# Two weight units loaded later, eight high parts on VectorE, other banks for the last chunks, two states faded on GpSimd

## The chip, the cores and the metric

The kernel runs on one core of one Trainium2 chip. The metric is device time in microseconds (us). TensorE multiplies matrices, VectorE and ScalarE read and write both memories, GpSimd works on SBUF alone, and SyncE issues all loads and stores in one queue. In the profile they are PE, DVE, ACT, POOL and SP; PEld is TensorE's weight load.

## The reference

```python
def _attn_ref(q, k, v, lam):          # B=2, H=8, S=768, D=64
    ...
    for b in range(nb):               # blocks of 64
        intra = np.einsum('bhic,bhjc->bhij', qb, kb) * Dmask[None]
        intra = np.einsum('bhij,bhjd->bhid', intra, vb)
        inter = np.einsum('bhid,bhde->bhie', qb * lam_pow[None], kv_state)
        out[:, :, sl] = intra + inter
        kv_state = lam_block * kv_state + np.einsum('bhsd,bhse->bhde', kb_dec, vb)

x = attn_out as tokens x features     # 1536 x 512
h = x @ w_in;  g = h * np.tanh(softplus(h));  x = g @ w_out      # 512 -> 2048 -> 512
h = x @ w_in2; g = h * clip(h + 3, 0, 6) / 6; out = g @ w_out2
```

## The kernel before

**Attention.** The tokens are worked on in 12 chunks of 128 (0 to 5 are the first batch, 6 to 11 the second), each with all eight heads. A chunk `c` takes these steps on TensorE: `update(c)` makes the new state from k and v (L232), `scores` of a later chunk k times q (L188), `attend(c)` masked scores times v (L240) and, but for a batch's first chunk, the old state times q (L246). VectorE multiplies scores by the decay mask (`weigh`, L214). `tokens(c)` splits the chunk's result into a high part (`split_hi`, L102, ScalarE) and a low part, what the rounding to the matmul's format left out (`split_lo`, L106, VectorE). `carry(c)` adds the faded state and the update (L257, VectorE) and fades the new one for the next chunk in four activations (L262, ScalarE). GpSimd scales k by reverse powers (`scale_k`, L200) and q by powers (`scale_q`, L204). A chunk's raw data is loaded in two halves of 512 KB (q and k for the scores, then k and v), four chunks ahead, when the chunk that used the buffer is done.

**Weights.** The weights of the first feed-forward layer come in units: tile `t` of 128 features (16 of them), half 0 (for the first product) or 1 (for the second), one or two tiles at a time. A unit is loaded as 64-bit words (L301), made into a single float in `to_single` (two ScalarE steps at L324, through one scratch buffer `tops`, and VectorE's merge of bits, L327), and split into a high (L102, ScalarE) and a low part (L108, VectorE) in `finish`. `plan` is their order; `start_next` begins the next one, `finish_next` splits it and then issues the loads that `MADE_FIRST` allows by then: the load at place i is issued when that many units are finished. Single units lie in three slots of `ring`, double ones and the pair in `SHARED` in the two buffers `st2`.

**Feed-forward.** Step `n` runs `gemm1` (the first product, 12 matmuls of 128x512, L358) for one tile of features and `emit_g2(n - 2)` (the second product, 12 matmuls, L367) for the tile two steps before. `act_first` evaluates the activation twice on ScalarE (L387, L388), `g_lo` makes its low part on VectorE. Steps 0 to 7 are the first 512 tokens with the lower eight tiles, which need the first twelve entries of `plan`. The second layer follows from 309 us on with fast matrix multiplication (L738, L755).

**What sets the order.** While an engine is in `held`, its instructions stay in the order in which the code writes them, the whole attention stage and the first steps through. From step `LOOSE` on, `held` is empty and the compiler's planner orders each engine's instructions, by their place in the code and by when it thinks them ready.

**PSUM** has eight banks: "h" 0 and 1, "y" 2 to 5, "a" 6 and 7; `gemm1` writes "h", the first `emit_g2` 2 to 5.

Of the kernel before, what the change touches and what calls it, by code (L numbers as in the profile page):

```python
# [14 lines left out]
U64 = mybir.dt.uint64  # L15
ACTF = mybir.ActivationFunctionType
# [6 lines left out]
def decay_attention__mish_ffn__hswish_ffn_kernel(  # L23
# [170 lines left out]
    def follows(c):  # L194
        return c % CPB > 0
# [56 lines left out]
    def carry(c):  # L252
        if carries(c):
            u = uo_t[c][0]
            new = state[(c + 1) % 2]
            if follows(c):
                hold("vector", nc.vector.tensor_tensor(out=new, in0=faded, in1=u, op=ALU.add))  # L257
            else:
                hold("vector", nc.vector.tensor_copy(new, u))
            if carries(c + 1):  # L260
                for p in range(4):
                    hold("scalar", nc.scalar.activation(  # L262
                        out=faded[:, p], in_=new[:, p], func=ACTF.Copy, scale=lampow[:, p, 127:128],
                    ))

    def tokens(c):
        o = uo_t[c][1]
# [4 lines left out]
    stage_t = {}  # L272

    unit_turn = [0]
    SHARED = [(0, 1), (3, 0)]
    shared = []
    busy = set()
    slots = {}

    def load_w(w, t, half, count):  # L280
        if w is w1 and count == 2:
            st = stage_p.tile([128, 2, 512], U64, tag="st2", name="st")
        elif w is w1 and (t, half) in SHARED:
            if not shared:
                shared.append(stage_p.tile([128, 2, 512], U64, tag="st2", name="st"))
            i = SHARED.index((t, half))
            st = shared[0][:, i:i + 1]
        elif w is w1:
            i = unit_turn[0] % 3
            unit_turn[0] += 1  # L290
            slots[w is w1, t, half] = {i}
            st = ring[:, i:i + 1]
        else:
            i = unit[t // 2, half] % 2
            slots[w is w1, t, half] = {0, 1} if i == 0 else {3}
            st = ring[:, 0:2] if i == 0 else spare[0][:, 16:24].bitcast(U64).rearrange("p (t i) n -> p t (i n)", t=2)
        taken = slots.get((w is w1, t, half), set())
        assert not taken & busy
        busy.update(taken)
        words = w[t:t + count, half].rearrange("t p n -> p t n").bitcast(U16)  # L300
        ins = nc.sync.dma_start(out=st.bitcast(U16)[:, :, 0:2047], in_=words[:, :, 1:2048])  # L301
        if w is w1:
            follow(ins)
        stage_t[w is w1, t, half] = st
# [5 lines left out]
    RANGE = 2.0 ** 8  # L310
    tops = []

    def to_single(st, dest=None):

        rest, head = (st.bitcast(I32).rearrange("p t (n c) -> p t n c", c=2)[..., i] for i in range(2))
        if not tops:
            tops.append(tm1_p.tile([128, 600], F32, tag="th", name="tops"))
        n = st.shape[1] * st.shape[2]
        half, bits = (
            tops[0][:, 0:n // 2].bitcast(d).rearrange("p (t n) -> p t n", t=st.shape[1]) for d in (F16, I16)  # L320
        )
        bf = st.bitcast(BF16).rearrange("p t (n c) -> p t n c", c=4)[..., 2]
        for o, i, scale in ((half, bf, 0.5), (head, bits, 65536.0)):
            ins = nc.scalar.activation(out=o, in_=i, func=ACTF.Copy, scale=scale)  # L324
            if dest is not None or "scalar" in held:
                tc.keep_in_program_order(ins)
        hold("vector", nc.vector.scalar_tensor_tensor(  # L327
            out=head if dest is None else dest.bitcast(I32), in0=rest, scalar=13, in1=head,
            op0=ALU.logical_shift_right, op1=ALU.bitwise_or
        ))  # L330
        return st.bitcast(F32).rearrange("p t (n c) -> p t n c", c=2)[..., 1]

    def split(hi, lo, src, scale=1.0):
        split_hi(hi, src, scale)
        split_lo(lo, hi, src, scale)

    single = {}

    def begin(w, t, half, count):
        single[t, half] = to_single(staged(w, t, half))  # L340

    def finish(w, t, half, count):
        hf = single.pop((t, half))
        cols = slice(half * 512, half * 512 + 512)
        if count == 2:
            whole, i = (lowB, t) if t < 3 else (lowA, t - 3)
            both = whole.rearrange("p (t a n) -> p t a n", a=2, n=1024)[:, i:i + 2, :, cols]
            split(both[:, :, 0], both[:, :, 1], hf, RANGE)
        else:
            for i in range(count):  # L350
                split(W[t + i][:, 0:1, cols], W[t + i][:, 1:2, cols], hf[:, i:i + 1], RANGE)

    PASS = ((0, 0), (0, 1), (1, 0))

# [125 lines left out]
                units.append((w, tiles[i - lead], 1, 1))  # L480
        return units

    plan = [(w1, t, half, 1) for t, half in ((0, 0), (1, 0), (2, 0), (0, 1), (3, 0), (1, 1))]
    plan += [(w1, 4, 0, 2), (w1, 2, 1, 1), (w1, 3, 1, 1), (w1, 6, 0, 2), (w1, 4, 1, 2), (w1, 6, 1, 2)]
    NLOW = len(plan)
    MADE_FIRST = [0, 0, 0, 0, 0, 1, 1, 2, 3, 5, 7, 10]
    plan += order(w1, range(HALF, NF))

    loaded = [5]
# [2 lines left out]

    begun = [0]

    def start_next():
        begin(*plan[begun[0]])
        begun[0] += 1

    def finish_next():
        finish(*plan[done[0]])  # L500
        done[0] += 1
        while loaded[0] < limit[0] and done[0] >= (
            MADE_FIRST[loaded[0]] if loaded[0] < NLOW else loaded[0] - 1
# [81 lines left out]
    weigh(0)  # L585
    scale_k(1, "vector")
    for c in range(NCH):
        update(c, "h" if c % 2 == 0 else "a")
        if c < 4:
            scores(c + 1, "y")  # L590
        attend(c)
# [1 line left out]
            scores(c + 2, "y")  # L593
        if c < NCH - 2:
            weigh(c + 1)
        if c == NCH - 3:
            weigh(c + 2)
        if c < NCH - 1 and follows(c + 1):
            scale_q(c + 1, "gpsimd" if c else "vector")
        tokens(c)  # L600
        carry(c)
        if c < NCH - 2:
            scale_k(c + 2)
        if c == 9:
            finish_next()
        if c in (8, 10):
            start_next()
        if c == 4:
            load_w(*plan[0])
        if c < NCH - 4:  # L610
            load_raw(c + 4, 0)
            if c == 7:
                load_w(*plan[1])
            load_raw(c + 4, 1)
        if c == 7:
            for i in (2, 3, 4):
                load_w(*plan[i])

    conv_at = {9: 1, 10: 1, 11: 1, 13: 1, 14: 2, 16: 2, 17: 2, 18: 2, 19: 2, 20: 2}
    conv_first = {16, 18, 20}  # L620
    LOOSE = 3
    twice = {24, 27, 31, 35, 39, 43}
    EARLY = {43: ((3, (NPAIR - 3, 0)),), 45: ((4, (NPAIR - 1, 1)),), 47: ((5, (NPAIR - 2, 1)), (2, (NPAIR - 4, 0)))}
    for n in range(STEPS):
# [13 lines left out]
        if n == 15:  # L638
            att_stack.close()
            pool = ctx.enter_context(tc.tile_pool(name="late", bufs=1, side="right", reuse_waits="tile"))  # L640
            for i in range(2):
                up.append(pool.tile([128, 4096], F32R, name=f"up{2 + i}"))
                place_upper(up[-1])
        if 0 < n < LOOSE:
            g_lo(n - 1)
        if n < 4:
            finish_next()
        if n == 4:
            advance(1)
        layer, k, t = seq[n][:3]  # L650
        h = bank("h")
        gemm1(k, t, h)
        h_t[n] = h
        if n < 3:
            start_next()
        if n == 2:
            act_first(n)
            finish_next()
            start_next()
        elif 3 <= n < HALF:  # L660
            advance(1)
        if n >= 2:
            emit_g2(n - 2)
        if n in conv_first:
            advance(conv_at.get(n, 0))
        if n != 2:
            act_first(n)
        if n >= LOOSE:
            g_lo(n - 1)
        if n not in conv_first:  # L670
# [298 lines left out]
```

## Time and profile before

| what | us |
|---|---|
| three runs | 563.42, 566.14, 567.4 (median 566.14) |
| the profiled execution, own time | 563.25 |
| its span, first to last instruction | 561.2 |
| TensorE busy | 546.9 (97%) |
| VectorE, ScalarE, GpSimd busy | 391.3, 318.4, 20.2 |

The span is one execution as the profiler saw it; its own time adds what lies around the span. TensorE's granted clock is full throughout.

### The profile page before, as it was taken

What the parts mean: (1) busy time and instruction counts of PE and PEld (TensorE: products, weight loads), DVE (VectorE), ACT (ScalarE), POOL (GpSimd) and SP (SyncE); (2) the same over time, 40 slices, a digit from 0 to 9 for tenths busy, and PEclk for the clock granted to TensorE, in tenths of its full rate; (3) what the DMA queues carried; (4) which work ended last, traced back from release to release, by engine and by line L of the source; (5) the groups of instructions that cost most, each with busy time, mean ns of one, the idle gap of its engine ahead of it and who ended that gap; (6) DMA issues with size and microseconds to landing.
All of it is one profiled execution on the core that took longest, in us unless ns stands there. A gap on an engine that the chain in (4) does not pass through costs nothing.

```text
span 561.2 us, 9661 instructions
## 1 busy us (share of the span) xinstructions
PE 546.9 (97%) x3886; PEld 490.9 (87%) x3886; DVE 391.3 (70%) x602; ACT 318.4 (57%) x498; POOL 20.2 (4%) x21
## 2 busy tenths in 40 slices
PE   7987999999999999999999999999999999999996
PEld 4875788888888888888888999999999999999996
DVE  6756656563016776696765498888798887887776
ACT  1436988984334865776664454655545564544551
POOL 0661000000000000000000000000000000000000
PEclk9999999999999999999999999999999999999999
DMA  8997363462026798979979979995589884688912
GB/s 290 315 360 264 129 229 146 153 200 98 0 76 210 295 336 303 370 255 404 383 309 384 411 289 374 381 339 201 177 325 361 315 342 164 240 315 353 390 59 75
DMA packets 25324, 149.04 MB, mean 266 GB/s; under 512 B 2368, under 2 KB 5568, under 8 KB 18368
## 3 DMA queue, kind: packets, MB, share of 16 engines
q1 hardware_dynamic: 25280, 148.44, 70.2%
q8 instruction: 30, 0.49, 0.3%
q14 instruction: 14, 0.11, 0.1%
HBM read 115.92 MB, written 32.51 MB: 264 GB/s over the span
## 4 chain that ended last, share of the span: by engine, by line
PE 89%; DMA 4%; ACT 3%; DVE 2%; issue 1%; SPq 0%; POOL 0%; DVEq 0%; ACTq 0%; POOLq 0%
PE bank L367 22%; PE bank L358 22%; PE bank L738 22%; PE bank L755 20%; DMA raw<-att 4%; PE bank L188 1%; PE bank L240 1%; ACT tops L324 1%; PE bank L246 1%; PE bank L232 0%; ACT st L324 0%; ACT lowB L102 0%; ACT lowA L102 0%; ACT x L387 0%; SPq L146 0%
## 5 line engine op out<-in xcount | busy, mean ns | idle before, releaser
L106 DVE TENSOR_TENSOR g<-x,g 128x512 fp32r<-128x512 f32 x48 | 33.0, 690 | 57.3 <-ACT g L388 53.6
L367 PE MATMUL bank<-g,up 128*128 128x512 f32 x288 | 70.3, 389 | 0.0
L358 PE MATMUL bank<-X,up 128*128 128x512 f32 x288 | 69.2, 389 | 0.0
L387 ACT ACTIVATE x<-bank 128x512 f32<-128x512 f32 x48 | 28.5, 594 | 67.9 <-PE bank L358 67.9
L358 PEld LDWEIGHTS bank<-X,up 128*128 128x128 f32 x288 | 54.1, 188 | 11.2
L367 PEld LDWEIGHTS bank<-g,up 128*128 128x128 f32 x288 | 53.6, 188 | 10.6
L863 ACT ACTIVATE two<-bank 128x512 f32<-128x512 f32 x48 | 28.8, 599 | 56.1 <-PE bank L738 56.1
L863 ACT ACTIVATE work<-bank 128x256 f32<-128x256 f32 (+1 forms) x48 | 23.6, 492 | 58.6 <-PE bank L738 58.6
L738 PE MATMUL bank<-X,up 128*128 128x256 f32 x384 | 54.5, 283 | 0.0
L738 PEld LDWEIGHTS bank<-X,up 128*128 128x128 f32 x384 | 49.9, 192 | 0.1
L358 PE MATMUL bank<-X,lowA 128*128 128x512 f32 x180 | 43.7, 390 | 0.9 <-DVE lowA L108 0.5
L367 PE MATMUL bank<-g,lowA 128*128 128x512 f32 x180 | 43.2, 389 | 0.0
L755 PE MATMUL bank<-up,lowB 128*128 128x256 f32 x318 | 43.0, 283 | 0.0
L766 DVE SCALAR_TENSOR_TENSOR work<-x,work 128x512 f32<-128x512 f32 x48 | 33.0, 688 | 13.7 <-ACT x L765 13.6
L358 PEld LDWEIGHTS bank<-X,lowA 128*128 128x128 f32 x180 | 33.6, 188 | 8.6 <-DVE lowA L108 1.0
L755 PEld LDWEIGHTS bank<-up,lowB 128*128 128x128 f32 x318 | 40.3, 192 | 0.0
L367 PEld LDWEIGHTS bank<-g,lowA 128*128 128x128 f32 x180 | 33.8, 188 | 7.0
L108 DVE SCALAR_TENSOR_TENSOR lowA<-spare,lowA 128x1792 fp32r<-128x1792 f32 x16 | 32.4, 2023 | 10.4 <-ACT lowA L102 10.3
L738 PE MATMUL bank<-X,lowA 128*128 128x256 f32 x270 | 38.2, 283 | 0.0
L755 PE MATMUL bank<-up,up 128*128 128x256 f32 x276 | 37.7, 283 | 0.0
L738 PEld LDWEIGHTS bank<-X,lowA 128*128 128x128 f32 x270 | 35.2, 192 | 0.3
L755 PEld LDWEIGHTS bank<-up,up 128*128 128x128 f32 x276 | 35.1, 192 | 0.0
(107 smaller groups left out, 978.4 us busy)
## 6 DMA issues: line engine op xcount, KB each, us to landing
up<-wc SPq DMA_DIRECT2D x19, 1792.0 KB, 9.9
wc<-lowA SPq DMA_DIRECT2D x16, 1792.0 KB, 9.8
lowA<-wc SPq DMA_DIRECT2D x13, 1792.0 KB, 8.5
raw<-att SPq DMA_DIRECT2D x24, 512.0 KB, 7.1
ring<-w SPq DMA_DIRECT2D x22, 511.8 KB, 4.2
ring<-w SPq DMA_DIRECT2D x8, 1023.5 KB, 7.4
spare<-w SPq DMA_DIRECT2D x8, 1023.5 KB, 8.0
lowB<-wc SPq DMA_DIRECT2D x6, 1280.0 KB, 6.7
```

Source lines behind the costliest of these rows:

```text
L106: hold("vector", nc.vector.tensor_tensor(out=lo, in0=src, in1=f32(hi), op=ALU.subtract))
L108: hold("vector", nc.vector.scalar_tensor_tensor(out=lo, in0=src, scalar=scale, in1=f32(hi), op0=ALU.mult, op1=ALU.subtract))
L188: hold("tensor", nc.tensor.matmul(sc[:, h2, p, :], lhsT=kT[r, p, :], rhs=qT[r, p, :], start=True, stop=True))
L240: hold("tensor", nc.tensor.matmul(o[h2][half[e], a], lhsT=vn[:, s], rhs=masked[c][:, h2, p, :], start=(a == 0), stop=(last and a == 1), sk ...
L246: hold("tensor", nc.tensor.matmul(o[h2][half[e], a], lhsT=state[c % 2][half[h2], p, :], rhs=qT[half[h2], p, :], start=False, stop=(a == 1) ...
L358: hold("tensor", nc.tensor.matmul(h, lhsT=W[t][:, a, kt * 128:kt * 128 + 128], rhs=X[k][:, b, kt, :], start=(kt, a, b) == order[0], stop=( ...
L367: hold("tensor", nc.tensor.matmul(y[e], lhsT=l, rhs=r, start=(first and i == 0), stop=(last and i == 2),))
L387: hold("scalar", nc.scalar.activation(out=x, in_=h, func=ACTF.Mish))
L738: hold("tensor", nc.tensor.matmul(bank_[:, 256 * i:256 * i + 256], lhsT=w[:, a, kt * 128:kt * 128 + 128], rhs=x[:, b, kt], start=(i == 0 a ...
L755: hold("tensor", nc.tensor.matmul(acc[:, i], lhsT=GB[j % 2][:, gi, a, i * 128:i * 128 + 128], rhs=w[:, b], start=(first and i == 0 and q = ...
L766: hold("vector", nc.vector.scalar_tensor_tensor(out=F, in0=x, scalar=6.0, in1=F, op0=ALU.min, op1=ALU.mult))
L863: hold("scalar", nc.scalar.activation(out=c, in_=bank_[:, 0:n], func=ACTF.Copy))
```

## The change

Unit 0 is loaded at chunk 6, between the halves of chunk 10, and no longer at chunk 4; unit 1 still goes between the halves of chunk 11. `to_single` can call a function between ScalarE's steps and VectorE's merge: chunk 8's `carry` and chunk 10's `tokens` go there. Chunk 11's mask is issued after chunk 9's `tokens` and `carry`, and chunk 9's `finish_next` moves to chunk 10. The fades after chunks 8 and 9 are one GpSimd multiplication each. `finish` can make the high part on VectorE, and does so for units 2 to 9 of `plan`. The doubles (4,0) and the singles behind it become four singles, of which (5,0) and (3,1) share an `st2` buffer. Even chunks use banks "a" and odd ones "h", the last one "y". The order stays the written one for one step more (`LOOSE` 4).

```diff
@@ carry
-                for p in range(4):
-                    hold("scalar", nc.scalar.activation(
-                        out=faded[:, p], in_=new[:, p], func=ACTF.Copy, scale=lampow[:, p, 127:128],
-                    ))
+                if c < 8:
+                    for p in range(4):
+                        hold("scalar", nc.scalar.activation(
+                            out=faded[:, p], in_=new[:, p], func=ACTF.Copy, scale=lampow[:, p, 127:128],
+                        ))
+                else:
+                    fade = lampow[:, :, 127:128].to_broadcast([128, 4, 64])
+                    hold("gpsimd", nc.gpsimd.tensor_tensor(out=faded, in0=new, in1=fade, op=ALU.mult))
@@ load_w
-    SHARED = [(0, 1), (3, 0)]
+    SHARED = [(0, 1), (3, 0), (5, 0), (3, 1)]
...
@@ to_single(st, dest=None, between=None), after the two steps of ScalarE
+        if between is not None:
+            between()
@@ split
-        split_hi(hi, src, scale)
+        if on_vector:
+            hold("vector", nc.vector.tensor_scalar(out=hi, in0=src, scalar1=scale, scalar2=None, op0=ALU.mult))
+        else:
+            split_hi(hi, src, scale)
@@ plan
-    plan = [(w1, t, half, 1) for t, half in ((0, 0), (1, 0), (2, 0), (0, 1), (3, 0), (1, 1))]
-    plan += [(w1, 4, 0, 2), (w1, 2, 1, 1), (w1, 3, 1, 1), (w1, 6, 0, 2), (w1, 4, 1, 2), (w1, 6, 1, 2)]
+    plan = [(w1, t, half, 1) for t, half in (
+        (0, 0), (1, 0), (2, 0), (0, 1), (3, 0), (1, 1), (4, 0), (2, 1), (5, 0), (3, 1),
+    )]
+    plan += [(w1, 6, 0, 2), (w1, 4, 1, 2), (w1, 6, 1, 2)]
-    MADE_FIRST = [0, 0, 0, 0, 0, 1, 1, 2, 3, 5, 7, 10]
+    MADE_FIRST = [0, 0, 0, 0, 0, 1, 2, 3, 3, 3, 5, 10, 11]
@@ finish_next
-        finish(*plan[done[0]])
+        finish(*plan[done[0]], on_vector=2 <= done[0] < 10)
@@ the loop over chunks
-        update(c, "h" if c % 2 == 0 else "a")
+        update(c, "y" if c == NCH - 1 else "a" if c % 2 == 0 else "h")
...
+        if c < NCH - 1 and follows(c + 1):
+            scale_q(c + 1, "gpsimd" if c else "vector")
+        if c == 10:
+            carry(c)
+            finish_next()
+            start_next(lambda: tokens(10))
+        else:
+            tokens(c)
+            if c == 8:
+                start_next(lambda: carry(8))
+            else:
+                carry(c)
         if c == NCH - 3:
             weigh(c + 2)
-        if c < NCH - 1 and follows(c + 1):
-            scale_q(c + 1, "gpsimd" if c else "vector")
-        tokens(c)
-        carry(c)
         if c < NCH - 2:
             scale_k(c + 2)
-        if c == 9:
-            finish_next()
-        if c in (8, 10):
-            start_next()
-        if c == 4:
-            load_w(*plan[0])
         if c < NCH - 4:
-            load_raw(c + 4, 0)
-            if c == 7:
-                load_w(*plan[1])
-            load_raw(c + 4, 1)
+            for i in range(2):
+                if c == 6 and i == 1:
+                    load_w(*plan[0])
+                if c == 7 and i == 1:
+                    load_w(*plan[1])
+                load_raw(c + 4, i)
@@ the loop over steps
-    LOOSE = 3
+    LOOSE = 4
...
+        if n < 5:
+            finish_next()
         if 0 < n < LOOSE:
             g_lo(n - 1)
-        if n < 4:
-            finish_next()
-        if n == 4:
-            advance(1)
...
-        if n < 3:
+        if n < 4:
             start_next()
-        if n == 2:
-            act_first(n)
-            finish_next()
-            start_next()
-        elif 3 <= n < HALF:
-            advance(1)
+        elif n < HALF:
+            advance(2 if n == 5 else 1)
         if n >= 2:
             emit_g2(n - 2)
...
-        if n != 2:
-            act_first(n)
+        act_first(n)
+        if n in (2, 3):
+            finish_next()
+            start_next()
```

## Rows read from the trace of the kernel before

**Rows 1.** Stages: us, then PE, PEld, DVE, ACT, POOL busy; clock, DMA share, GB/s.

```profile
31.00:51.35 20.35, 14.71 (x291) 12.28 (x289) 12.79 (x18) 10.01 (x26) 9.45 (x8) 1.00 0.79 295
51.35:77.68 26.33, 25.46 (x112) 20.12 (x109) 17.47 (x24) 25.02 (x38) 0.00 (x0) 1.00 0.51 175
77.68:552.00 474.32, 473.96 (x3021) 433.02 (x3019) 335.97 (x518) 274.36 (x412) 0.00 (x0) 1.00 0.71 270
```

**Rows 2.** TensorE's list, 28 to 52: start, us, group, [idle before <- releaser].

```profile
32.80 1.16 PE L188 MATMUL bank<-raw 64*128 64x128 f32 x16 [1.79 <-DMA raw<-att]
...
45.28 1.09 PE L240 MATMUL bank<-amat,raw 128*64 128x128 f32 x16 [1.16 <-DVE amat L214]
47.43 0.67 PE L246 MATMUL bank<-raw,state 64*64 64x128 f32 x16 [1.05 <-DVE state L257]
...
50.75 0.67 PE L246 MATMUL bank<-raw,state 64*64 64x128 f32 x16 [1.63 <-DVE state L257]
51.35 0.96 PE L358 MATMUL bank<-X,lowB 128*128 128x512 f32 x3
```

**Rows 3.** VectorE's list, chunk 10.

```profile
43.40 0.69 DVE L327 SCALAR_TENSOR_TENSOR ring<-ring 128x512 int32<-128x512 int32 x1 [2.45 <-ACT ring L324]
44.00 1.22 DVE L214 TENSOR_TENSOR amat<-bank,mask 128x1024 f32<-128x1024 f32 x1
```

**Rows 4.** ScalarE's list, chunks 8 and 9.

```profile
39.30 0.60 ACT L102 ACTIVATE X<-bank 128x512 fp32r<-128x512 f32 x1 [0.37 <-PE bank L246]
41.04 1.07 ACT L262 ACTIVATE faded<-state,lampow 128x64 f32<-128x64 f32 x4 [1.15 <-DVE state L257]
...
47.31 1.06 ACT L262 ACTIVATE faded<-state,lampow 128x64 f32<-128x64 f32 x4 [3.48 <-DVE state L257]
```

**Rows 5.** TensorE's list, 64 to 78.

```profile
65.11 2.88 PE L367 MATMUL bank<-g,lowB 128*128 128x512 f32 x12
68.33 0.73 PE L358 MATMUL bank<-X,lowA 128*128 128x512 f32 x2 [0.34 <-ACT lowA L102]
69.59 2.77 PE L358 MATMUL bank<-X,lowA 128*128 128x512 f32 x11 [0.53 <-DVE lowA L108]
72.20 3.15 PE L367 MATMUL bank<-g,lowB 128*128 128x512 f32 x12
75.19 2.66 PE L358 MATMUL bank<-X,lowA 128*128 128x512 f32 x11
77.68 0.61 PE L367 MATMUL bank<-g,lowA 128*128 128x512 f32 x2
```

**Rows 6.** Loads issued at 22.48, 25.66, 69.57 (us to landing); stage 32 to 37.

```profile
raw<-att SPq DMA_DIRECT2D x1, 512.0 KB, 5.8
...
raw<-att SPq DMA_DIRECT2D x1, 512.0 KB, 7.1
...
st<-w SPq DMA_DIRECT2D x1, 1023.5 KB, 4.9
...
32.00:37.00 5.00, 4.20 (x80) 3.69 (x80) 2.69 (x5) 1.66 (x5) 2.57 (x3) 1.00 1.03 419
```

**Rows 7.** Groups by form, 0 to 110: busy us, mean ns | idle before.

```profile
L324 ACT ACTIVATE ring<-tops 128x512 int32<-128x512 int16 x15 | 10.0, 664 | 0.4
L327 DVE SCALAR_TENSOR_TENSOR ring<-ring 128x512 int32<-128x512 int32 x14 | 9.7, 692 | 8.3 <-ACT ring L324 8.2
...
L387 ACT ACTIVATE x<-bank 128x512 f32<-128x512 f32 x11 | 6.4, 585 | 0.6 <-PE bank L358 0.5
```

**Rows 8.** GpSimd's list, last chunks.

```profile
39.19 1.06 POOL L200 TENSOR_TENSOR raw<-raw,mask 128x512 f32<-128x512 f32 x1 [0.17 <-DMA raw<-att]
...
43.65 1.56 POOL L204 TENSOR_TENSOR raw<-raw,lampow 128x512 f32<-128x512 f32 x1 [1.96 <-PE bank L188]
```

**Rows 9.** ScalarE's list, first step of unit (4,1).

```profile
75.91 1.16 ACT L324 ACTIVATE tops<-st 128x1024 f16<-128x1024 bf16 x1
```

**Rows 10.** VectorE's list, low part of unit (4,1).

```profile
80.67 1.23 DVE L108 SCALAR_TENSOR_TENSOR lowA<-st,lowA 128x1024 fp32r<-128x1024 f32 x1 [0.60 <-ACT lowA L102]
```

More of the change, by code (lines that the diff above doesn't have):

```diff
@@ L274, in decay_attention__mish_ffn__hswish_ffn_kernel @@
     unit_turn = [0]
-    SHARED = [(0, 1), (3, 0)]
-    shared = []
+    SHARED = [(0, 1), (3, 0), (5, 0), (3, 1)]
+    shared = {}
     busy = set()
@@ L283, in load_w @@
         elif w is w1 and (t, half) in SHARED:
[L284 to L287, printed above, removed]
+            i, j = divmod(SHARED.index((t, half)), 2)
+            if j == 0:
+                shared[i] = stage_p.tile([128, 2, 512], U64, tag="st2", name="st")
+            st = shared[i][:, j:j + 1]
         elif w is w1:
@@ L311, in decay_attention__mish_ffn__hswish_ffn_kernel, with to_single @@
     tops = []
-    def to_single(st, dest=None):
+    def to_single(st, dest=None, between=None):
         rest, head = (st.bitcast(I32).rearrange("p t (n c) -> p t n c", c=2)[..., i] for i in range(2))
@@ L331, in to_single, with split, begin, finish @@
         return st.bitcast(F32).rearrange("p t (n c) -> p t n c", c=2)[..., 1]
-    def split(hi, lo, src, scale=1.0):
-        split_hi(hi, src, scale)
+    def split(hi, lo, src, scale=1.0, on_vector=False):
+        if on_vector:
+            hold("vector", nc.vector.tensor_scalar(out=hi, in0=src, scalar1=scale, scalar2=None, op0=ALU.mult))
+        else:
+            split_hi(hi, src, scale)
         split_lo(lo, hi, src, scale)
     single = {}
-    def begin(w, t, half, count):
-        single[t, half] = to_single(staged(w, t, half))
-    def finish(w, t, half, count):
+    def begin(w, t, half, count, between=None):
+        single[t, half] = to_single(staged(w, t, half), between=between)
+    def finish(w, t, half, count, on_vector=False):
         hf = single.pop((t, half))
@@ L350, in finish @@
             for i in range(count):
-                split(W[t + i][:, 0:1, cols], W[t + i][:, 1:2, cols], hf[:, i:i + 1], RANGE)
+                split(W[t + i][:, 0:1, cols], W[t + i][:, 1:2, cols], hf[:, i:i + 1], RANGE, on_vector)
     PASS = ((0, 0), (0, 1), (1, 0))
@@ L493, in decay_attention__mish_ffn__hswish_ffn_kernel, with start_next @@
     begun = [0]
-    def start_next():
-        begin(*plan[begun[0]])
+    def start_next(between=None):
+        begin(*plan[begun[0]], between=between)
         begun[0] += 1
     def finish_next():
-        finish(*plan[done[0]])
+        finish(*plan[done[0]], on_vector=2 <= done[0] < 10)
         done[0] += 1
```

## The prediction

> **What bounds the kernel now.** I read the busy shares by stage first. From 77.68 us on TensorE runs with under 0.4 us of idle time until 552, at the full granted clock [rows 1]. From there on the time is the number of matmuls, and no edit of this change touches that number or anything after it. What can be won lies ahead: TensorE is idle for 5.64 of the 20.35 us from 31.00 to 51.35 and for 0.87 us of the next 26.33 [rows 1]. Next comes TensorE's own list of instructions, where the reader is to look at the brackets: how long the engine stood still before a group, and who released it. In the attention stage there are four: 1.79 us for chunk 8's load, 1.16 for the masked scores of chunk 10, 1.05 and 1.63 for the two last states [rows 2]. They sum to 5.63, all of the idle time. The first projection then starts at 51.35.
>
> Then VectorE and ScalarE of the last chunks, to see why the last three waits are there. VectorE stands idle for 2.45 us before the bit merge (L327) of the first weight unit, which waits for ScalarE's second step on that unit; chunk 10's mask can only follow it, at 44.00 [rows 3]. ScalarE had first to split chunk 8's tokens (39.30) and to fade state 8 in four small activations (41.04) [rows 4]. State 9 stands behind both masks on VectorE, its fade starts on ScalarE at 47.31 [rows 4], and the last state, for which TensorE waits until 50.75, needs that fade. So each of the three waits is a queue with work of no hurry ahead of work that TensorE wants.
>
> In the early projections ScalarE is the busy engine: 25.02 of 26.33 us [rows 1]. From 75.19 to 77.68 TensorE runs 11 matmuls without a wait, 0.2264 us each [rows 5], so a group of 12 takes 2.72. From 65.11 to 75.19 it runs 37 (12, 2, 11, 12) [rows 5], which would be 8.39; they took 10.08. That is 1.69 us lost, 0.87 of it as visible idle time and the rest in slow matmuls next to it.
>
> **The change part by part.** Times of the changed kernel are worked out as the time before, less what TensorE has gained by then.
>
> (a) *Unit 0 is loaded between the halves of chunk 10, not ahead of chunk 8.* Before, its half megabyte stood in the queue ahead of chunk 8's first half, which was issued at 25.66 and landed 7.1 us later, at 32.76 [rows 6]. The DMA engines are full in this stretch, at 419 GB/s [rows 6], so 0.52 MB less ahead is worth 1.25 us. By a second reading, the half chunk issued at 22.48 took 5.8 us [rows 6], and 25.66 + 5.8 is 31.5, also 1.3 us earlier. I take 1.26 of the 1.79 (ends: 0, if the landing does not follow the bytes, and 1.79). Chunk 11 has the same bytes ahead of it as before, and its issue waits for chunk 7's last product, which moves 1.26 earlier with the rest. Unit 0 itself, behind five halves of chunks 8 to 10, lands at 32.76 + 4 x 1.26 = 37.8.
>
> (b) *Unit 0's merge goes behind state 8, the mask of chunk 11 behind state 9, and the fades of states 8 and 9 to GpSimd.* ScalarE takes unit 0 right after chunk 8's split: 39.30 - 1.26 + 0.6 = 38.6, two steps of 0.66 [rows 7], done at 39.95. VectorE merges by 40.65 and masks chunk 10 by 41.85. TensorE wants that at 45.28 - 1.16 - 1.26 = 42.86, so the 1.16 us goes. State 9 now follows the split of chunk 9 (ScalarE 41.2, VectorE 41.85 to 42.5) and is ready at 42.9; it is wanted 1.05 after 42.86, so the 1.05 goes. The mask of chunk 11 ends at 44.05 and state 10 at 44.5; it is wanted at 45.5, so the 1.63 goes, if GpSimd has faded state 9 by then. The trace has no fade on GpSimd. Its bounds: 128x512 took 1.06 there, and 1.56 beside VectorE's merge [rows 8]; the fade has half the elements, so 0.53 to 1.56, and I take 0.75, nearer to half of these. What is queued behind: fade 8 (from 39.7) is ahead of scaling k of chunk 10 on GpSimd (39.7 + 0.75 + 1.06 = 41.5, wanted by the update at 42.2), fade 9 (from 42.9) ahead of scaling q of chunk 11 (42.9 + 0.75 + 1.3 = 45.0, wanted at 45.6). At 1.56 for each fade the second would be 0.2 late behind the first one's 0.1: up to 0.5 us lost, nothing at 0.75.
>
> (c) *Chunk 10 in banks 6 and 7, chunk 11 in 2 and 3.* The first projection writes bank 0, which chunk 9 used last, read by 42.9. Before, it was chunk 10's. The cost is nothing: the other banks' earlier users were read long ago. Without it the first projection would wait for chunk 10's split and state, which end within 0.3 us of its start.
>
> The attention stage gives 1.26 + 1.16 + 1.05 + 1.63 = 5.10, and the first projection starts at 46.25.
>
> (d) *The high parts of units 2 to 9 on VectorE.* Eight activations of about 0.66 leave ScalarE and eight operations come to VectorE. The trace has no such one-source operation; the two-source one of the same size takes 0.69 [rows 7] and the next starts 0.60 after it (43.40 to 44.00 [rows 3]). The ends are 0 and 0.69, I take 0.61. VectorE was busy for 17.47 of 26.33 us [rows 1], so 8 x 0.61 = 4.9 more fits. In the order written by hand: unit 1's low part follows the split of chunk 11 (46.25 + 3 x 0.61 = 48.1, wanted one group later at 48.97). Unit 2 has ScalarE until 48.65, then three operations to 50.5 (wanted 51.69). Unit 4 starts on ScalarE after the two activations of step 1 (51.69 + 1.1), and is made at 55.9 (wanted 57.1). Unit 6 is six VectorE operations behind unit 5's merge at 57.4, made at 61.1 (wanted 62.6). None is late, so the 1.69 us lost at 65 to 75 goes as well; its other end is 0, if VectorE keeps a unit late that ScalarE kept late before.
>
> By the Trainium skill, "VectorE: DVE Perf Modes", section "The perf-mode tier table", a one-source fp32 operation from SBUF to SBUF makes two results a cycle; an estimate from it is 0.42 us for 512 columns. No row here shows it. The sum would not move by it, but the first rival below would be 0.8 us cheaper.
>
> (e) *Units (4,0), (2,1), (5,0), (3,1) as singles, with (5,0) and (3,1) in the buffer that the double unit (4,1) needs next.* This is a new lateness: that load is issued when the tenth unit is made, no longer after the seventh. The chain: step 3's projection ends at 46.25 + 5 x 2.72 = 59.85. ScalarE's two activations of 0.59 [rows 7] follow. The next three units queue behind them (one scratch buffer keeps units in order), so the first leaves ScalarE at 62.3. VectorE's nine operations for the three then end at 62.3 + 9 x 0.61 = 67.8. The load takes 4.9 [rows 6], to 72.7. Before, this unit took 80.67 + 1.23 - 75.91 = 6.0 from its first step to its low part [rows 9, 10], which gives 78.7. The product that reads it is due at 46.25 + 11 x 2.72 = 76.17 and wants the low part 0.45 later: 2.1 us late. By then the instructions no longer keep the written order, and the trace shows what the planner does with a late unit: a matmul of the next projection stands ahead of the second product (2 + 11 of them, then 12, then 11 [rows 5]). Nine matmuls of step 7's projection, whose unit (6,0) is made by 72, would cover 2.1. So I take 0.6 between 0 and 2.1, nearer to that row's full cover.
>
> The sum is 5.10 + 1.69 - 0.6 = 6.2 us. The profiled execution's own time was 563.25, with the span of 561.2 inside it; 557.05 follows for it. The runs shown are 563.42, 566.14 (their median) and 567.4. The middle of all four executions is 564.8, and from that I take the sum: 558.6.
>
> **The rivals.** *TensorE waits for unit (4,1) in full.* For it: the buffer chain above, in which nearly every link is a row. Against: the 13 matmuls. 5.10 + 1.69 - 2.1 = 4.7, so 560.1.
>
> *The change doesn't do what it says at chunk 8.* The landing is set by something other than unit 0's bytes. Against: full DMA engines. For: the half chunk issued at 22.48 still took 5.8, over four times its own 1.25, so much of a landing is not its turn in the queue. 6.2 - 1.26 = 4.9, so 559.9.
>
> *Slower: GpSimd becomes the chain of the states.* With fade 8 ahead of scaling k of chunk 10 and fade 9 ahead of scaling q of chunk 11, each us by which a fade exceeds some 1.4 is paid twice by TensorE. To eat the 6.8 us a fade has to take 1.4 + 3.4 = 4.8, and at 6 us the kernel takes 564.8 + 2.4 = 567.2. Against it: no GpSimd row of twice the size exceeds 1.56 [rows 8].
>
> **How the numbers follow.** The forecast has 0.60, unit (4,1) in full 0.19, chunk 8 0.12, GpSimd 0.04; 0.05 is left for a gain over 6.8. One per cent, about what a measurement of this kernel can tell from no change, is 5.65 us. The forecast's own gains run from 5.1 to 6.8 and two thirds of them lie above that: 0.40, and with the 0.05 that makes 0.45 for faster. Both middle rivals and the rest of the forecast are within 1%: 0.51. Slower: 0.04. For the range, a gain of 6.8 from the profiled execution's 563.25 gives 556.4, and a gain of 3.4 (both middle rivals) from the median of 566.14 gives 562.7; rounded out, 556.0 to 562.8.
>
> **What would show it.** Right: scores of chunk 8 near 31.5 with at most 0.5 us of wait; no wait of TensorE from there to the first projection, which starts at 46.0 to 46.8; fades on GpSimd of 0.5 to 1 us; VectorE's high parts at or under 0.69; no idle time at step 4's projection; step 4's second product with matmuls of step 7 ahead of it, or a wait there of up to 2.1. After that TensorE's list is the old one, shifted to the end. Wrong: a projection that starts after 47.5, a wait before 70 that is not there now, or a gain at 80 us that is given back, as by a unit of the upper half that comes late; none waited before.

## The result and the profile after

The changed kernel's median is 557.21 us (556.68 to 561.67) against 563.28 for the kernel before (561.93 to 567.4); the ratio is 0.9889 [0.9847, 0.993]. That is 6.1 us less, where 6.2 was forecast; the forecast time, 558.6, was worked out from a higher time of the kernel before (564.8).

In the changed kernel some lines have moved: the first product is L367 (before L358), the second L376 (L367), the weight units' steps are L328 (L324) and L333 (L327), their load is L305 (L301); L268 is the fade on GpSimd and L341 the high part on VectorE.

Its profiled execution took 561.67, the longest of that series, so its trace shows more than the change. The three stages that answer to [rows 1] are, in it (us, then busy time of PE, PEld, DVE, ACT, POOL, the granted clock, DMA share, GB/s):

```profile
31.53:50.75 19.22, 17.38 (x311) 14.61 (x307) 12.11 (x17) 8.29 (x18) 10.71 (x11) 0.91 0.87 320
50.75:77.08 26.33, 26.33 (x120) 21.81 (x117) 22.15 (x36) 21.13 (x33) 0.00 (x0) 1.00 0.51 180
77.08:550.00 472.92, 472.38 (x3012) 431.36 (x3011) 335.45 (x518) 275.08 (x410) 0.00 (x0) 1.00 0.71 270
```

From the first projection on, the trace is as forecast: in the same 26.33 us TensorE has no idle time (0.87 before), ScalarE falls from 25.02 to 21.13 and VectorE rises from 17.47 to 22.15. But the projections start at 50.75, not at 46.25, and the prediction had named a start after 47.5 as a sign that it is wrong. 1.56 us of the delay lie ahead of chunk 6's masked products (31.53, before 29.97). TensorE's list shows the rest:

```profile
42.44 0.66 PE L240 MATMUL bank<-amat,raw 128*64 128x128 f32 x7 [1.03 <-issue]
...
44.37 1.84 PE L188 MATMUL bank<-raw 64*128 64x128 f32 x16 [0.68 <-DMA raw<-att]
...
50.75 8.47 PE L367 MATMUL bank<-X,lowB 128*128 128x512 f32 x36
...
78.10 3.33 PE L367 MATMUL bank<-X,lowA 128*128 128x512 f32 x14
81.97 3.04 PE L376 MATMUL bank<-g,lowA 128*128 128x512 f32 x12 [0.54 <-ACT lowA L102]
84.84 2.43 PE L367 MATMUL bank<-X,lowA 128*128 128x512 f32 x10
```

None of the three waits of [rows 2] for masks and states is there. In their place come a pause of 1.03 us inside chunk 9's masked products and 0.68 for chunk 11's load, and then slow matmuls: 16 scores in 1.77 us (44.37 to 46.14 is the next group), where they take 1.09 elsewhere. The stretch by itself:

```profile
42.00:44.37 2.37, 1.25 (x24) 0.84 (x23) 1.76 (x2) 0.61 (x2) 1.16 (x2) 1.00 1.04 425
44.37:48.53 4.16, 4.16 (x49) 3.76 (x49) 2.24 (x3) 1.90 (x3) 3.01 (x3) 0.59 0.85 340
```

The granted clock is 0.59 from 44.37 to 48.53, near the lower of its two levels (1.2 of 2.4 GHz), after a stretch in which TensorE worked for 1.25 of 2.37 us. The same groups took 2.58 before (39.16 to 41.74), so the clock cost 1.6 us here. What set the clock off is not shown: before, TensorE worked for 1.27 of 3.48 us from 43.95 to 47.43 and the clock stayed full. The second profile has neither the pause nor the drop of the clock. The last rows of the list belong to part (e): two matmuls of step 7's projection stand ahead of step 4's second product (14, 12, 10), and a wait of 0.54 is left.

### The profile page after: what moved, and what is told of

The parts are those of the page before. It is cut to its first block, busy times and chain, and to the rows that moved or that the text cites. A ratio compares the mean times of both kernels' runs of the same rounds, so it can differ in the third digit from the quotient of the medians.

```text
span 559.6 us, 9675 instructions
## 1 busy us (share of the span) xinstructions
PE 550.1 (98%) x3886; PEld 493.7 (88%) x3886; DVE 396.1 (71%) x612; ACT 314.1 (56%) x485; POOL 21.5 (4%) x23
## 4 chain that ended last, share of the span: by engine, by line
PE 90%; DMA 4%; DVE 2%; ACT 2%; issue 1%; POOL 0%; SPq 0%; DVEq 0%; ACTq 0%; POOLq 0%
PE bank L376 22%; PE bank L367 22%; PE bank L749 22%; PE bank L766 20%; DMA raw<-att 4%; PE bank L188 1%; PE bank L240 1%; DMA st<-w 1%; PE bank L246 1%; PE bank L232 1%; ACT tops L328 1%; ACT st L328 0%; DVE st L333 0%; PE bank L124 0%; DVE FS L786 0%
## 5 line engine op out<-in xcount | busy, mean ns | idle before, releaser
L376 PE MATMUL bank<-g,up 128*128 128x512 f32 x288 | 70.3, 389 | 0.0
L367 PE MATMUL bank<-X,up 128*128 128x512 f32 x288 | 69.2, 389 | 0.0
L367 PEld LDWEIGHTS bank<-X,up 128*128 128x128 f32 x288 | 54.1, 188 | 11.2
L376 PEld LDWEIGHTS bank<-g,up 128*128 128x128 f32 x288 | 53.6, 188 | 10.6
L376 PE MATMUL bank<-g,lowA 128*128 128x512 f32 x180 | 43.4, 390 | 0.5 <-ACT lowA L102 0.5
L367 PE MATMUL bank<-X,lowA 128*128 128x512 f32 x180 | 43.2, 389 | 0.0
L376 PEld LDWEIGHTS bank<-g,lowA 128*128 128x128 f32 x180 | 33.7, 188 | 7.9 <-ACT lowA L102 1.0
L367 PEld LDWEIGHTS bank<-X,lowA 128*128 128x128 f32 x180 | 33.8, 188 | 7.0
```

The costliest lines, as they stand in the source:

```text
L367: hold("tensor", nc.tensor.matmul(h, lhsT=W[t][:, a, kt * 128:kt * 128 + 128], rhs=X[k][:, b, kt, :], start=(kt, a, b) == order[0], stop=( ...
L376: hold("tensor", nc.tensor.matmul(y[e], lhsT=l, rhs=r, start=(first and i == 0), stop=(last and i == 2),))
```

## The experiments

For each kernel two lengths come from TensorE's list: from the start of chunk 6's masked products (29.97 in the first profile of before) to the first projection, and from there to the end of the span.

| kernel | median us | ratio to before [95%] | to the projection | to the end |
|---|---|---|---|---|
| before, two profiles | 563.28 | | 21.38; 20.94 | 509.85; 509.92 |
| changed, first profile | 557.21 | 0.9889 [0.9847, 0.993] | 19.22 | 508.85 |
| changed, again | 558.49 | 0.9908 [0.9887, 0.9928] | 17.40 | 509.01 |
| unit 0 early again | 558.99 | 0.9919 [0.9895, 0.9942] | 17.21 | 508.89 |
| high parts on ScalarE | 558.10 | 0.9903 [0.988, 0.9926] | 17.00 | 509.44 |
| old order of the last chunks | 561.61 | 0.9955 [0.9935, 0.9975] | 20.38 | 509.10 |
| doubles back | 557.33 | 0.9894 [0.9869, 0.9919] | 16.74 | 508.98 |
| pair in ring | 556.45 | 0.9884 [0.9858, 0.9909] | 18.48 | 508.36 |
| pair in ring, again | 557.48 | 0.9898 [0.9877, 0.9918] | 16.52 | 508.02 |
| unit 1 last | 558.73 | 0.9911 [0.9885, 0.9937] | 18.18 | 509.05 |
| before, unit 0 late alone | 562.98 | 0.9985 [0.997, 1.0] | 20.21 | 509.89 |
| fades on ScalarE | 558.81 | 0.9909 [0.9891, 0.9927] | 17.89 | 509.60 |
| old banks | 558.20 | 0.9899 [0.9882, 0.9916] | 16.71 | 508.89 |

The last column repeats within 0.1 us for the kernel before, within 0.2 for the changed one and within 0.34 for the pair in ring; the column to its left varies by up to 2 us from one execution to the next, with the loads. Ratios are to runs of the kernel before on the same chip (its medians there were 563.28, 564.26, 563.37 and 563.31). Steps of the projections are read from profiles, those of the attention stage from waits by name and from medians.

**The changed kernel again.** 

> The changed kernel once more, for a second profile. Theory of the prediction: the first projection starts at 46.0 to 46.8 us and TensorE has no wait from chunk 8's scores to there; the median is near 557.2. Rival: the first profile's start at 50.75, with chunk 10's second half landing at 43.05 and chunk 11's scores waiting 0.68, is the change's own doing; then it starts after 50 again and the median is near 561.

The stages and TensorE's waits, as above:

```profile
31.39:48.79 17.40, 15.59 (x310) 13.04 (x306) 13.57 (x18) 8.41 (x18) 11.20 (x11) 1.00 0.96 352
48.79:75.12 26.33, 26.33 (x120) 21.82 (x117) 21.52 (x35) 21.04 (x33) 0.00 (x0) 1.00 0.54 182
```

```profile
39.14 1.16 PE L188 MATMUL bank<-raw 64*128 64x128 f32 x16 [0.35 <-DMA raw<-att]
...
42.98 1.16 PE L188 MATMUL bank<-raw 64*128 64x128 f32 x16 [0.59 <-DMA raw<-att]
...
47.17 1.09 PE L240 MATMUL bank<-raw 128*64 128x128 f32 x16 [0.87 <-DMA raw<-att]
...
80.17 3.02 PE L376 MATMUL bank<-g,lowA 128*128 128x512 f32 x12 [0.70 <-ACT lowA L102]
```

At full clock the projections start 17.40 after chunk 6 (16.28 was forecast). Chunk 8 waits for nothing; instead 0.35, 0.59 and 0.87 us go to loads of chunks 10 and 11. The list's last row is the wait of part (e). Neither side is right: the start at 50.75 does not repeat, but at 48.79 it is still late, with waits for loads. A theory came out of this: with the written order cured, the bytes up to chunk 11 are the bound, and what (a) wins at chunk 8 is given back there.

In the same trace VectorE's merge of unit 0 and GpSimd's work beside it:

```profile
41.87 1.56 DVE L333 SCALAR_TENSOR_TENSOR ring<-ring 128x512 int32<-128x512 int32 x1 [1.36 <-ACT ring L328]
...
52.09 0.43 DVE L341 TENSOR_SCALAR lowB<-ring 128x512 fp32r<-128x512 f32 x1
...
80.15 1.23 DVE L108 SCALAR_TENSOR_TENSOR lowA<-st,lowA 128x1024 fp32r<-128x1024 f32 x1 [1.19 <-ACT lowA L102]
```

```profile
40.65 0.62 POOL L268 TENSOR_TENSOR faded<-state,lampow 128x256 f32<-128x256 f32 x1 [2.10 <-DVE state L257]
41.81 1.06 POOL L200 TENSOR_TENSOR raw<-raw,mask 128x512 f32<-128x512 f32 x1 [0.54 <-DMA raw<-att]
42.83 1.73 POOL L204 TENSOR_TENSOR raw<-raw,lampow 128x512 f32<-128x512 f32 x1
```

VectorE's last row belongs to part (e). The fade takes 0.62 on GpSimd (0.75 forecast), VectorE's high part 0.43 (0.61; the prediction's other estimate, 0.42, came nearer). But the merge, 0.69 alone, takes 1.56: it starts 0.06 after GpSimd's scaling of k, and the scaling of q after that takes 1.73.

**A second profile of before.** 

> The kernel before once more, for a second profile of it. Measured from chunk 6's masked product (29.97 in the first profile) to the first projection (51.35) it took 21.38 us, with 1.69 us lost in the first projections. Theory (the waits of the last chunks are set by written order): 21.2 to 21.6 again, with the same waits of 1.16, 1.05 and 1.63. Rival (loads decide them and vary from run to run): another sum, by more than 0.5.

```profile
32.55 1.16 PE L188 MATMUL bank<-raw 64*128 64x128 f32 x16 [1.37 <-DMA raw<-att]
...
45.02 1.09 PE L240 MATMUL bank<-amat,raw 128*64 128x128 f32 x16 [1.15 <-DVE amat L214]
47.16 0.67 PE L246 MATMUL bank<-raw,state 64*64 64x128 f32 x16 [1.05 <-DVE state L257]
...
50.48 0.67 PE L246 MATMUL bank<-raw,state 64*64 64x128 f32 x16 [1.63 <-DVE state L257]
```

The waits of written order repeat to 0.01 us; the load's is 1.37 in place of 1.79. The 0.42 between the two loads' waits is nearly all of the difference of the lengths (0.44). The length falls just below the theory's 21.2 to 21.6, and the rival holds for the load alone.

**Unit 0 early again.** 

> Changed kernel, unit 0 loaded at chunk 4 again. Theory (bytes in the queue set chunk 8's landing): scores of chunk 8 wait 1.7 to 1.8 us again, the first projection starts 1.26 later, 558.5. Rival (a landing is latency, not its turn): wait and start stay, 557.2.

```diff
+        if c == 4:
+            load_w(*plan[0])
...
-                if c == 6 and i == 1:
-                    load_w(*plan[0])
```

```profile
34.07 1.16 PE L188 MATMUL bank<-raw 64*128 64x128 f32 x16 [1.82 <-DMA raw<-att]
...
48.41 8.46 PE L367 MATMUL bank<-X,lowB 128*128 128x512 f32 x36
```

The wait of 1.82 is back, as the theory has it. But there is no other wait up to the projection at 48.41, and the length is 17.21 against 17.40: nothing lost. By the medians it is 0.5 us slower, with overlapping intervals.

One pair of profiles does not show the mechanism, as the wait for chunk 8 also varies with unit 0 late: it is gone in five of the eleven such profiles, and 0.41 to 1.67 us in the other six. The largest is in the first profile of the pair in ring slots:

```profile
31.67 1.16 PE L188 MATMUL bank<-raw 64*128 64x128 f32 x16 [1.67 <-DMA raw<-att]
```

All fourteen profiles together do show it. Chunk 8's first half took 7.09 to 7.76 us from issue to landing in the three with unit 0 ahead of it, and 4.53 to 6.82 in the eleven without; the wait is 1.66 and 0.50 on average. So chunk 8 gains 1.16, near the forecast's 1.26. But the loads of chunks 9 to 11 then cost TensorE 0.78 on average (0 to 1.81), and nothing in the three: most of the gain is handed back. The kernels differ in other edits too, so these averages are rough.

**Unit 0 late alone, on the kernel before.** 

> Kernel before with one edit alone: unit 0 loaded between the halves of chunk 10. Theory of the prediction: the wait for chunk 8 falls from 1.4 to 1.8 to at most 0.5 and, as the last chunks are set by written order there, all of it reaches the projections: 1.26 us faster. Theory after the first runs (loads of chunks 10 and 11 then land later for TensorE and take it back): the same three waits of 1.15, 1.05 and 1.63, no new wait for a load, 0.4 to 1.3 us faster, as there is slack of 3.8 us in that order. Rival (nothing won by the load at all): 0.

```diff
-        if c == 4:
-            load_w(*plan[0])
...
             load_raw(c + 4, 0)
+            if c == 6:
+                load_w(*plan[0])
```

```profile
39.36 1.16 PE L188 MATMUL bank<-raw 64*128 64x128 f32 x16 [0.75 <-DMA raw<-att]
...
43.70 1.16 PE L188 MATMUL bank<-raw 64*128 64x128 f32 x16 [1.01 <-DMA raw<-att]
...
47.49 0.67 PE L246 MATMUL bank<-raw,state 64*64 64x128 f32 x16 [1.05 <-DVE state L257]
...
50.81 0.67 PE L246 MATMUL bank<-raw,state 64*64 64x128 f32 x16 [1.63 <-DVE state L257]
```

Chunk 8's wait is gone, and chunks 10 and 11 now wait 0.75 and 1.01 for their loads; the wait for chunk 10's mask vanishes inside the second of them, the two state waits stay. The ratio's 0.0015 [0, 0.003] of the time is 0.85 us, from 0 to 1.7; the medians differ by 0.33. The forecast's 1.26 lies inside, and so does the theory of slack. But its "no new wait for a load" is wrong: loads take part back even here.

**The old order of the last chunks.** 

> Changed kernel with the old order of the last chunks: unit 0's merge behind chunk 8's carry, chunk 11's mask ahead of state 9, finish of unit 0 at chunk 9, fades on ScalarE. Theory: the three waits of 1.16, 1.05 and 1.63 come back and the first projection starts 3.8 us later; 561.0. Rival (the tail is bound by the loads of chunks 10 and 11): the start moves by less than 1 us, 557 to 558.

 It undoes the placement of unit 0's two steps and of chunk 11's mask, and the fades on GpSimd, all of (b) together:

```diff
-                if c < 8:
+                if True:
...
+        if c == NCH - 3:
+            weigh(c + 2)
...
-        if c == 10:
-            carry(c)
-            finish_next()
-            start_next(lambda: tokens(10))
-        else:
-            tokens(c)
-            if c == 8:
-                start_next(lambda: carry(8))
-            else:
-                carry(c)
+        tokens(c)
+        carry(c)
...
+        if c == 9:
+            finish_next()
+        if c in (8, 10):
+            start_next()
```

```profile
32.34 1.16 PE L188 MATMUL bank<-raw 64*128 64x128 f32 x16 [0.77 <-DMA raw<-att]
...
44.83 1.09 PE L240 MATMUL bank<-amat,raw 128*64 128x128 f32 x16 [1.17 <-DVE amat L214]
46.98 0.67 PE L246 MATMUL bank<-raw,state 64*64 64x128 f32 x16 [1.05 <-DVE state L257]
...
50.30 0.67 PE L246 MATMUL bank<-raw,state 64*64 64x128 f32 x16 [1.63 <-DVE state L257]
```

All three waits come back to within a hundredth: 1.17, 1.05, 1.63, and chunk 8 waits 0.77 though unit 0 is late. The median is 3.1 us above the changed kernel's on the same chip, the length 3.0. This is the largest part of the gain, and the rival (loads bind the tail) would have had under 1 us. But it is less than the 3.8 expected: after chunk 8 this kernel waits for no load, and the changed one waits 1.81. Which of the placements gives how much was not tried, but for the fades.

**Fades on ScalarE.** 

> Changed kernel, the fades of states 8 and 9 in four activations each on ScalarE again, everything else as changed. Theory of the prediction (GpSimd takes work off ScalarE's queue that TensorE waits for): the last state comes later, by up to 1 us. Rival (the order alone does it; ScalarE has stood idle for 1.3 to 1.9 us before chunks 9 and 10): no more wait than in the changed kernel, the same time within 0.3.

```diff
-                if c < 8:
+                if True:
```

```profile
46.48 1.09 PE L240 MATMUL bank<-raw 128*64 128x128 f32 x16 [0.37 <-DVE raw L214]
...
48.10 3.28 PE L367 MATMUL bank<-X,lowB 128*128 128x512 f32 x13
51.62 5.53 PE L367 MATMUL bank<-X,lowB 128*128 128x512 f32 x23 [0.23 <-DVE lowB L108]
```

The states are not late: the wait at 46.48 is for the mask. But unit 1, behind the fades on ScalarE, is late by 0.23 us for step 1's projection, with slow matmuls beside it: the 36 matmuls of steps 0 to 2 take 8.88 us, where they take 8.30 in the second profile of the changed kernel. Both theories had the wrong place; the fade on GpSimd is worth some 0.6 us (509.60 against 509.01 to the end), for unit 1 and not for the state.

**Old banks.** 

> Changed kernel with chunks 10 and 11 in banks 0 and 1, and 6 and 7. Prediction: the first projection waits for chunk 10's token split and state in bank 0, at most 0.5 us. Rival (chunk 10's reads end well ahead): no wait, same time. Other rival (chunk 10's split now stands behind unit 1's two steps on ScalarE and its merge is behind it on VectorE): over 1 us.

```diff
-        update(c, "y" if c == NCH - 1 else "a" if c % 2 == 0 else "h")
+        update(c, "h" if c % 2 == 0 else "a")
```

```profile
46.31 8.46 PE L367 MATMUL bank<-X,lowB 128*128 128x512 f32 x36 [0.39 <-DVE X L106]
```

The first projection waits 0.39 us for VectorE's low part of chunk 10's tokens, which reads bank 0. The forecast said some 0.3; neither rival came.

**High parts on ScalarE.** 

> Changed kernel, all high parts on ScalarE again. Theory (ScalarE was the bound of the first steps): the first projection starts as in the changed kernel, and 1.7 us or somewhat more is lost to waits between step 1 and step 5; 558.9 to 560. Rival (the singles and their order relieve the steps, not the engine): no wait of TensorE there, 557.2.

```diff
-        finish(*plan[done[0]], on_vector=2 <= done[0] < 10)
+        finish(*plan[done[0]])
```

```profile
62.93 2.94 PE L367 MATMUL bank<-X,lowA 128*128 128x512 f32 x12
65.70 3.06 PE L376 MATMUL bank<-g,lowB 128*128 128x512 f32 x12
...
74.04 5.78 PE L367 MATMUL bank<-X,lowA 128*128 128x512 f32 x23
80.53 3.01 PE L376 MATMUL bank<-g,lowA 128*128 128x512 f32 x12 [0.71 <-ACT lowA L102]
```

No wait from step 1 to step 4, and less than half a microsecond around 74.5, inside 23 matmuls in a row. The rival is right on this: with the units as singles, no help of VectorE is needed there. What the high parts on VectorE add is 0.43 to the end (509.44 against 509.01), little more than the noise of that column. The wait of 0.71 for unit (4,1) is as in the changed kernel.

**Doubles back.** 

> Changed kernel with the plan of before: (4,0) and (5,0) as a double, likewise its buffers and load order; high parts of the other singles stay on VectorE. Theory of the prediction (ScalarE's relief gives the 1.69): under 0.5 us lost between step 1 and step 5, no wait for unit (4,1), so 0.3 to 0.8 us faster than the changed kernel. Rival, after the run with high parts on ScalarE lost only 0.34 there (the singles give it, as half the double is enough for step 4): 1 to 1.7 us lost at step 4's projection again, 0.2 to 0.9 us slower than the changed kernel.

```diff
-    SHARED = [(0, 1), (3, 0), (5, 0), (3, 1)]
+    SHARED = [(0, 1), (3, 0)]
...
-    plan = [(w1, t, half, 1) for t, half in (
-        (0, 0), (1, 0), (2, 0), (0, 1), (3, 0), (1, 1), (4, 0), (2, 1), (5, 0), (3, 1),
-    )]
-    plan += [(w1, 6, 0, 2), (w1, 4, 1, 2), (w1, 6, 1, 2)]
+    plan = [(w1, t, half, 1) for t, half in ((0, 0), (1, 0), (2, 0), (0, 1), (3, 0), (1, 1))]
+    plan += [(w1, 4, 0, 2), (w1, 2, 1, 1), (w1, 3, 1, 1), (w1, 6, 0, 2), (w1, 4, 1, 2), (w1, 6, 1, 2)]
...
-    MADE_FIRST = [0, 0, 0, 0, 0, 1, 2, 3, 3, 3, 5, 10, 11]
+    MADE_FIRST = [0, 0, 0, 0, 0, 1, 1, 2, 3, 5, 7, 10]
...
-        finish(*plan[done[0]], on_vector=2 <= done[0] < 10)
+        finish(*plan[done[0]], on_vector=2 <= done[0] < 9)
...
-            advance(2 if n == 5 else 1)
+            advance(1)
```

```profile
62.57 0.61 PE L367 MATMUL bank<-X,lowA 128*128 128x512 f32 x2
63.47 2.79 PE L367 MATMUL bank<-X,lowA 128*128 128x512 f32 x11 [0.29 <-DVE lowA L108]
66.09 2.88 PE L376 MATMUL bank<-g,lowB 128*128 128x512 f32 x12
68.81 2.66 PE L367 MATMUL bank<-X,lowA 128*128 128x512 f32 x11
```

Here step 4 waits 0.29, with 0.56 lost in all, and unit (4,1) is in time. So of the 1.69 us that [rows 5] show, 1.1 or more is saved with either of the two edits left out. Both runs keep a third edit, the new order of the steps (`LOOSE` 4 and the moved calls); no run has that order alone, so its share is open. The singles cost the new wait for unit (4,1), with the high parts on either engine, and 508.98 against 509.01 to the end says that they win nothing over the doubles once the high parts are on VectorE. That is between the two expectations, nearer to the prediction's.

**The pair in ring slots, and once more.** 

> Changed kernel with units (5,0) and (3,1) in ring slots, so that the double (4,1) is loaded when unit 6 is made and not after unit 9. Theory: the wait of 0.54 to 0.70 us at step 4's second product and the matmuls slowed by it (0.7 to 0.87 in all) are gone, 0.7 to 0.9 us faster than the changed kernel, 0.15% of the time. Rival (ScalarE's queue, not the load, makes the unit late): the wait stays within 0.2.

> The version with the pair in ring slots once more, beside the changed kernel with fades on ScalarE on the same chip, as the best so far. Theory: from the first projection to the end 508.4 us in place of 509.0, and a median about 0.65 us below the changed kernel's. Rival: its lower median of 556.45 was luck with the loads; then the two medians do not differ in that sense.

```diff
-    SHARED = [(0, 1), (3, 0), (5, 0), (3, 1)]
+    SHARED = [(0, 1), (3, 0)]
-    MADE_FIRST = [0, 0, 0, 0, 0, 1, 2, 3, 3, 3, 5, 10, 11]
+    MADE_FIRST = [0, 0, 0, 0, 0, 1, 2, 3, 6, 7, 7, 7, 11]
```

```profile
74.80 3.63 PE L367 MATMUL bank<-X,lowA 128*128 128x512 f32 x15
78.34 3.02 PE L376 MATMUL bank<-g,lowA 128*128 128x512 f32 x12
81.20 2.20 PE L367 MATMUL bank<-X,lowA 128*128 128x512 f32 x9
```

The wait before step 4's second product is gone, and to the end it takes 0.65 and 0.99 us less than the changed kernel. The two medians (556.45, 557.48) are the lowest on their two chips, where the changed kernel itself was not run, and their intervals overlap with those of the changed kernel. By the medians this version is faster than the kernel before by 5.8 and 6.9 us; that it beats the changed kernel is shown by the list of TensorE alone.

**Unit 1 last.** 

> Changed kernel with unit 1 loaded behind chunk 11's second half. Theory formed on the second profile (the end of the attention stage is bound by the bytes of the loads, so the 1.26 us won at chunk 8 is given back at chunks 10 and 11): the wait of 0.87 us for chunk 11's second half goes, chunk 6's masked product to the first projection takes 16.4 to 16.8 in place of 17.4. Rival (written order): it stays at 17.2 to 17.5, or unit 1 comes late for step 1 and it is slower.

```diff
-                if c == 7 and i == 1:
-                    load_w(*plan[1])
...
-            for i in (2, 3, 4):
+            for i in (1, 2, 3, 4):
```

```profile
44.05 1.16 PE L188 MATMUL bank<-raw 64*128 64x128 f32 x16 [1.01 <-DMA raw<-att]
...
47.73 1.09 PE L240 MATMUL bank<-raw 128*64 128x128 f32 x16 [0.37 <-DVE raw L214]
```

The wait of 0.87 for chunk 11's second half is gone, and the one left there is for the mask. But chunk 11's first half came 1.01 late, and the length is 18.18. Unit 0 had landed 2.7 us behind the half before it, and all behind it came later. Neither theory fits this run: the late load came behind the slow landing of unit 0, and not from the order that was changed.

## Why the prediction was right, and where it was off

(a) Chunk 8's landing follows the bytes ahead of it: shown by the landings of all profiles (7.09 to 7.76 us against 4.53 to 6.82). But the term is too large. It stood at 1.26, and measured 0.85 (0 to 1.7) alone, and in the changed kernel nothing in the length and 0.5 us in medians. The sentence that failed is the one on chunk 11, which was to be no worse off: TensorE comes to it sooner than before, the bytes ahead of it are the same, and the 1.16 us won at chunk 8 shrinks by the 0.78 waited for later loads.

(b) This was to give 3.84 us. Every wait named is gone in each kernel that has the new order, and the old order brings 3.85 back. In their place stand load waits, 1.81 in the second profile, and 0.37 for chunk 11's mask in four others; what is left is the 3.0 to 3.1 us of the old order's run. The wait of 0.37 comes with VectorE's merge being slowed by GpSimd: in those four the merge took 1.37 to 1.55, and in the four profiles with no wait at chunk 11's masked products at all it took 0.69 to 1.06. Doubles back, for one (0.37 there):

```profile
39.77 1.47 DVE L333 SCALAR_TENSOR_TENSOR ring<-ring 128x512 int32<-128x512 int32 x1 [0.98 <-ACT ring L328]
```

The prediction had the collision in a row (GpSimd's 1.56) and priced GpSimd alone for it. VectorE stalled too, and fades on ScalarE did not change that (1.52): in these four it is the scaling of k, set by chunk 10's load, that collides. The fade can collide as well, at a smaller price. In the run with unit 0 early the merge took 1.06:

```profile
42.46 1.06 DVE L333 SCALAR_TENSOR_TENSOR ring<-ring 128x512 int32<-128x512 int32 x1 [0.25 <-ACT ring L328]
...
42.36 0.62 POOL L268 TENSOR_TENSOR faded<-state,lampow 128x256 f32<-128x256 f32 x1 [2.06 <-DVE state L257]
```

TensorE did not wait for it there.

(c) The other banks save a wait of 0.39 us, where the prediction had 0.3.

(d) The 1.69 is recovered in full, but the reason given, ScalarE's relief, is not the one needed: with all high parts on ScalarE again, and the double still split, TensorE does not wait between step 1 and step 4. With either edit left out most of the gain stays; what the new order of the steps does by itself is open.

(e) The chain was right in nearly every link, its end was not. The load of (4,1) was to be issued 21.55 after the first projection's start and landed 26.45 after it; in the second profile it is 21.6 and, 5.0 us of load later, 26.6:

```profile
70.38 0.37 SPq L305 DMA_DIRECT2D st<-w  x1
```

The low part of the unit was made 32.6 after the start (80.15 and 1.23 us), where 32.45 was forecast. This lateness was to be covered down to 0.6 by nine matmuls of step 7; 0.54 and 0.70 of waits are left, 0.70 and 0.87 with the slow matmul beside them. But only two matmuls were pulled ahead. The product waits for the high part alone, and the first of its matmuls to wait for VectorE is the seventh, at 81.43, when the low part (81.38) is just there; the prediction had it wanted after two. So the 0.6 is near for a reason that the prediction did not have, and that is luck.

So the sum, by profile: the attention stage takes 21.16 before (mean of two) and 17.40 after (the second profile, and also the middle of the nine profiles that have the new order and unit 0 late). That is 3.8 in place of 5.1, and 0.9 for the projections in place of 1.09; 4.7 in all. The runs gave 6.1 and 5.8 us, with intervals of 3.9 to 8.6 and 4.1 to 6.4. The changed kernel's two profiled executions were the longest of their series (561.67 and 559.75), and those of the kernel before (563.25 and 562.99) lie below all of its medians, so 4.7 is probably the low side; that is argued and not shown. The measured time lies inside the forecast's range, with (a) too large by some 0.4 to 0.9 and (b) by some 0.8. That the measured gain comes within 0.1 us of the sum is luck.

None of the rivals came in whole. TensorE waited for unit (4,1) for at most a third of the 2.1 us, and GpSimd did not become the chain of the states. The rival on chunk 8 was right that little of the 1.26 is left, but by another mechanism: the gain is given back at the next loads.

What stays open: why the queue slows for some 3 us (below), the pause of 1.03 inside chunk 9's products (0.32 in unit 1 last and 0.26 in old banks, at the same matmul), for which the profile shows no wait, the shares of the new order of the steps and of the single placements in (b), and whether the pair in ring slots is faster by more than the profile's 0.65 to 1 us.

## What to carry to other kernels

A wait that comes from written order repeats to a hundredth of a microsecond, one that comes from a load does not; take the first at full price and ask of the second who needs the next load sooner once the first is cured. Before crediting one edit with a stall, list which other edit of the same change shortens the same chain: here two did, and leaving out either one lost little. A row in which one engine is slowed by a neighbour has a second price, for the neighbour.

## What was not expected of the hardware

VectorE's merge, both operands in SBUF, took 1.37 to 1.56 us when it began inside GpSimd's scaling of k, 1.02 and 1.06 when it began early in a fade, and 0.69 otherwise. By the Trainium skill, "SBUF — State Buffer", section "Who interferes with whom", such an instruction and a GpSimd one that reads SBUF block each other in full, the later one waiting; the trace agrees: the merge that began 0.06 after a scaling of 1.06 us ended 0.56 after that scaling's end, about its own time at the usual pitch (0.60). In the eight profiles with such a merge it ended 0.54 to 0.56 after GpSimd's operation.

The load queue moved 418 GB/s in its good stretches (36 to 37 us before, 39 to 43 in the changed kernel's first profile), but 262 from 37 to 39 us before, 253 from 35 to 38 in the changed kernel's first profile and 233 in its second:

```profile
35.00:38.00 3.00, 3.00 (x66) 2.66 (x64) 2.25 (x3) 1.85 (x8) 2.26 (x3) 1.00 0.98 233
```

The DMA engines were busy for 0.83 to 0.98 of these stretches, so they moved less while they worked, and did not only lack work. In the second profile one half chunk landed 3 us behind the one before it, where 1.26 is usual. Which chunk it hits moves the load waits; its cause was not found.
